# The second half of w_out, loaded behind a transpose instead of ahead of it

## The chip, the core and the metric

The kernel runs on one core of a Trainium2 chip. The metric is device time in microseconds (us): the time of one execution of the whole kernel on that core. A core has a matrix engine (TensorE, "PE" in the profile, with its weight loads as "PEld"), VectorE (DVE), ScalarE (ACT), GpSimd (POOL), and SyncE (SP), which in this kernel only issues transfers. Sixteen DMA engines move the data[...].

## The reference

The input x has 8 sequences of 4096 tokens with 192 channels. First comes a causal convolution over 7 tokens, with softmaxed taps that differ by head (8 heads of 24 channels). Then a two-layer network with the gate h * cos(h):

```
w   = softmax(weight)                          # 8 heads x 7 taps
c[s]= sum_k w[head, k] * x[s - 6 + k]          # zeros before a sequence starts
h   = c @ w_in                                 # 192 -> 2048
g   = h * cos(h)
out = g @ w_out                                # 2048 -> 192
```

All 32768 tokens go through it. The output is float32.

## The kernel before

The tokens are cut into 32 units of 1024 and, for the network, into 64 tiles of 512 (two tiles to a unit). For one unit the work is: load x (`load_unit`, L72, and `load_edges`, L68, both on SP's queue); cast it to bf16 (`cast_unit`, L178, mostly on GpSimd); convolve by matmuls with a banded matrix (`conv_mm`, L191) and copy the result to `ct` (`conv_out`, L200); transpose `ct` to `cT`, channels on the partitions, with a DMA transpose on SP's queue (`turn_unit`, L263); put right the first 6 tokens of each block (`mend_edges`, L283). The network then reads `cT`. In unit 0 the first half is transposed on TensorE (`turn_first`, L350) so that tile 0 can start early; its second half, which tile 1 reads, goes through the DMA transpose.

For one tile, `mm1` (L387) makes eight blocks of h, each 256 of the 2048 channels in a PSUM buffer of which there are three (`h_pool`). `gcu` (L399) has ACT compute the cosine (as a sine, L402) and DVE the product `g` (L406), after which the PSUM buffer is free again. `mm2_step` (L412) multiplies `g` by w_out (L439). It runs one tile behind `mm1`: during tile 1 it works on tile 0, and from its 17th step on it uses the second half of w_out.

w_out comes in float32 in two halves of two transfers each, 384 KB per transfer (`load_wo`, L94, on SP's queue), and each half is cast to bf16 on GpSimd (`cast_wo`, L91).

The order on TensorE is written out by hand, one string for a tile (`PE_FIRST` for the first four, then `PE_ORDER`), with `ACT_FIRST` and `ACT_ORDER` for ACT. "h3" is the fourth block of h, "m5" five steps of the second product, "c1 c2" and "d1 d2" parts of the convolution of later units, "r" the convolution of unit 0's second half:

```
PE_FIRST = ["h0a h0b h1 h2 h3 r h4 h5 d1 d2 h6 h7 c1 c2",
            "p h0 m5 h1 m5 h2 m6 h3 m12 h4 m2 h5 m2 q d1 d2 m5 h6 m6 c1 c2 m3 h7 m3",
```

In tile 1, d1 is the convolution of unit 2. "er" in ACT's string of tile 0 is the copy of "r" to `ct`; behind it stand the transpose of unit 0's second half and then, on SP, the loads of unit 2:

```
                    if k == "er":
                        turn_unit(0, NB, UB)
                        load_unit(2)
                        load_edges(2)
                        cast_wo(0)
```

After tile 0's string come, in program order, the copy of unit 1's `ct` (`double_unit`, L254), `cast_wo(1)`, the loads of unit 3 and the cast of unit 2. The transpose of unit 1 is issued in tile 1. SP works its list off in program order and stands where an entry waits; GpSimd does the same with its casts.

## Time and profile before

The time is 713.3 us, the median of three (713.25, 713.30, 715.74). The profiled execution spans 714.0 us.

| Engine | busy us | share of the span |
|---|---|---|
| TensorE (PE) | 703.3 | 99% |
| VectorE (DVE) | 646.7 | 91% |
| ScalarE (ACT) | 590.4 | 83% |
| GpSimd (POOL) | 300.9 | 42% |

| Transfers on SP's queue | count | KB each |
|---|---|---|
| x, whole units | 30 | 768 |
| x, half units | 4 | 384 |
| x, edges | 31 | 96 |
| w_out | 4 | 384 |
| transposes ct to cT | 32 | not listed |
| out | 63 | 384 |

A line of the timeline reads: start, duration, engine, line of the kernel, operation, output <- inputs, shape, count, and in brackets the idle time before it and what ended that. A line of the chain reads: start, duration, what the chain was in. A busy PE in these records is not PE at its peak, since the ends of matmuls are modelled.

### The profile page before, as it was taken

The page shows a single profiled execution, that of the slowest core. Times are in us where ns is not written, and L with a number is a line of the kernel's source. Part 1 is how long each engine was busy: PE and PEld are TensorE (multiplying, and loading weights), DVE is VectorE, ACT ScalarE, POOL GpSimd, SP SyncE. Part 2 cuts the span into 40 slices and gives each one's busy share as a digit, 9 for nine tenths or more (in the row PEclk, how much of TensorE's full clock was granted, in tenths as well). Part 3 has the DMA queues.
Part 4 walks back from the last instruction along what each step waited for, and adds up shares of the span by engine and source line. Part 5 has one row for each costly group of instructions (what it writes and reads, how often), then busy time and mean ns, then how long its engine had stood idle before and what let it go on. Part 6 is the DMA issues. An engine that isn't in the chain of part 4 may idle for free.

```text
span 714.0 us, 26519 instructions
## 1 busy us (share of the span) xinstructions
PE 703.3 (99%) x11828; PEld 538.3 (75%) x11829; DVE 646.7 (91%) x601; ACT 590.4 (83%) x719; POOL 300.9 (42%) x307
## 2 busy tenths in 40 slices
PE   7899999999999999999999999999999999999997
PEld 3577777777777777777777777777777777777776
DVE  7799999999999999999999999999999999999995
ACT  7788888888888888888888888888888888888774
POOL 6553345553245533445543355534355533453200
PEclk9999999999999999999999999999999999999999
DMA  8954553545644535544546534445535565513402
GB/s 213 232 110 115 145 127 100 138 94 127 146 104 115 142 86 137 146 107 113 126 94 146 144 97 124 113 107 145 137 91 138 98 122 145 122 52 92 95 25 68
DMA packets 183713, 85.25 MB, mean 119 GB/s; under 512 B 111664, under 2 KB 183216, under 8 KB 183600
## 3 DMA queue, kind: packets, MB, share of 16 engines
q1 hardware_dynamic: 182888, 82.59, 48.3%
q8 instruction: 92, 1.51, 0.9%
q0 software_dynamic: 416, 0.79, 0.8%
q14 instruction: 21, 0.17, 0.1%
q10 hardware_dynamic: 296, 0.20, 0.1%
HBM read 31.36 MB, written 25.17 MB: 79 GB/s over the span
## 4 chain that ended last, share of the span: by engine, by line
PE 96%; DVE 1%; DMA 1%; ACT 1%; issue 0%; POOL 0%; POOLq 0%; SPq 0%
PE o_ps L439 47%; PE h L395 46%; PE h L194 3%; DMA cT<-ct 1%; DVE g L406 0%; ACT cs L402 0%; PE h L439 0%; DVE band L320 0%; POOL mask L131 0%; ACT mask L136 0%; ACT ct L343 0%; PE o_ps L194 0%; DVE diag L309 0%; DVE cT L361 0%; PE h L358 0%
## 5 line engine op out<-in xcount | busy, mean ns | idle before, releaser
L406 DVE TENSOR_TENSOR g<-h,cs 128x1024 bf16<-128x1024 f32 (+1 forms) x513 | 606.4, 1220 | 32.3 <-ACT cs L402 21.8
L402 ACT ACTIVATE cs<-h 128x1024 bf16<-128x1024 f32 (+1 forms) x513 | 511.9, 1026 | 102.2 <-PE h L395 68.2
L439 PEld LDWEIGHTS <-g 64*128 64x128 bf16 x8192 | 369.5, 94 | 91.2 <-issue 1.2
L439 PE MATMUL o_ps<-wo,g 64*128 64x192 bf16 x8128 | 434.9, 243 | 0.0
L395 PE MATMUL h<-cT,w 64*128 64x512 bf16 (+1 forms) x3078 | 413.7, 376 | 4.7 <-DVE g L406 2.5
L395 PEld LDWEIGHTS <-w 64*128 64x128 bf16 x3078 | 161.1, 94 | 72.4 <-issue 4.8
L292 POOL TENSOR_TENSOR edge_prod<-cT,tap 128x1008 f32<-128x1008 bf16 x30 | 67.2, 2239 | 347.0 <-DMA cT<-ct 347.0
L183 POOL CAST x_bf<-x_f 128x1728 bf16<-128x1728 f32 (+2 forms) x33 | 80.6, 2444 | 6.7 <-DMA x_f<-in_x_dram 6.7
L209 ACT CAST ct<-h 128x384 bf16<-128x384 f32 x120 | 51.8, 483 | 8.5 <-PE h L194 4.8
L450 DVE COPY o_sb<-o_ps 128x384 f32<-128x384 f32 x63 | 35.2, 558 | 23.6 <-PE o_ps L439 23.2
L258 POOL COPY ct<-ct 128x1536 bf16<-128x1536 bf16 (+1 forms) x31 | 45.6, 1472 | 3.4 <-ACT ct L209 3.4
L194 PE MATMUL h<-x_bf,band 64*128 64x192 bf16 (+1 forms) x472 | 41.0, 243 | 0.0
L297 POOL TENSOR_TENSOR edge_prod<-edge_prod 128x144 f32<-128x144 f32 x60 | 33.3, 554 | 4.7
L295 POOL TENSOR_TENSOR edge_prod<-edge_prod 128x432 f32<-128x432 f32 x30 | 30.3, 1009 | 2.4
L450 ACT COPY o_sb<-o_ps 128x384 f32<-128x384 f32 x63 | 29.8, 473 | 1.6 <-PE o_ps L439 1.6
L194 PEld LDWEIGHTS <-band 64*128 64x128 bf16 (+1 forms) x496 | 24.7, 94 | 2.1 <-issue 1.0
L298 POOL TENSOR_TENSOR cT<-edge_prod 128x144 bf16<-128x144 f32 x30 | 18.3, 608 | 2.4
L260 POOL COPY ct<-x_bf 128x192 bf16<-128x192 bf16 x60 | 19.2, 349 | 0.0
L108 PE MATMUL o_ps<-zero 128*128 128x512 bf16 x12 | 4.7, 554 | 1.3 <-DVE zero L103 1.3
L108 PEld LDWEIGHTS <-zero 128*128 128x128 bf16 x15 | 1.6, 121 | 3.3 <-issue 1.9
L460 DVE COPY o_sb<-h 128x192 f32<-128x192 f32 x1 | 0.4, 358 | 3.7 <-PE h L439 3.7
L460 ACT COPY o_sb<-h 128x192 f32<-128x192 f32 x1 | 0.3, 319 | 3.8 <-PE h L439 3.8
(62 smaller groups left out, 43.3 us busy)
## 6 DMA issues: line engine op xcount, KB each, us to landing
out_dram<-o_sb SPq DMA_DIRECT2D x63, 384.0 KB
x_f<-in_x_dram SPq DMA_DIRECT2D x30, 768.0 KB
x_f<-in_x_dram SPq DMA_DIRECT2D x31, 96.0 KB
x_f<-in_x_dram SPq DMA_DIRECT2D x4, 384.0 KB
wo_f<-in_moe_w_out_dram SPq DMA_DIRECT2D x4, 384.0 KB
w<-in_moe_w_in_dram POOLq DMA_DIRECT2D x2, 384.0 KB, 6.3
cT<-ct SPq DMA_TRANSPOSE x32
out_dram<-o_sb ACTq DMA_DIRECT2D x2, 96.0 KB
```

The lines of the kernel that those rows point to most:

```text
L183: copy(out=bf[u][:, n0 + o : n1 + o, :].rearrange("p n (h k r) -> p (n h) k r", k=NC, r=R), in_=x_tiles[u][:, n0:n1, :].rearrange("p n (h ...
L194: return nc.tensor.matmul(out=ps[i // 2][:, 0 : (n1 - n0) * 2 * G].rearrange("p (n k i r) -> p i n k r", n=n1 - n0, k=NC, i=2)[:, i % 2], ...
L209: copy(o[:, :, 0, :], i[:, :, 0, :])
L258: nc.gpsimd.tensor_copy(out=ct[:, 0:nb, :, 1, :], in_=ct[:, 0:nb, :, 0, :])
L292: nc.gpsimd.tensor_tensor(out=edge_prod, in0=window, in1=tap.rearrange("p (a b k) -> p a b k", a=1, b=1).to_broadcast([128, NC * UB, K - 1 ...
L295: nc.gpsimd.tensor_tensor(out=edge_prod[:, :, :, 0:3], in0=edge_prod[:, :, :, 0:3], in1=edge_prod[:, :, :, 3:6], op=ALU.add)
L297: nc.gpsimd.tensor_tensor(out=edge_prod[:, :, :, 0], in0=edge_prod[:, :, :, 0], in1=edge_prod[:, :, :, j], op=ALU.add)
L395: nc.tensor.matmul(out=h[:, i, n0 * 128 : n1 * 128], lhsT=w[rows, k, j, :], rhs=c[rows, m0 + n0 : m0 + n1, k, :], start=(k == 0), stop=(k ...
L402: nc.scalar.activation(out=cs[:, :, part], in_=h[:, :, part], func=AF.Sin, bias=math.pi / 2.0, scale=1.0)
L406: nc.vector.tensor_tensor(out=g_tiles[t][:, 2 * j : 2 * j + 2, part], in0=h[:, :, part], in1=cs[:, :, part], op=ALU.mult)
L439: ms.append(nc.tensor.matmul(out=o_ps[tt, b, si], lhsT=g_tiles[tt][rows, f, s * 128 : (s + 1) * 128], rhs=wo[rows, f // 2, f % 2, :], star ...
L450: copies[b](o_sb[t][:, 2 * b : 2 * b + 2, :].rearrange("p s d -> p (s d)"), o_ps.pop((t, b)))
```

## The change

`load_wo(1)`, the two transfers of w_out's second half, is taken from the end of `conv_first` (after the conv of unit 0's first half) and put directly behind the transpose of unit 0's second half. In SP's queue and in the rings it then stands behind that transpose and ahead of the loads of unit 2. It is for letting the transpose, which tile 1 waits for, go ahead of data that are needed later. What is computed and what is transferred stays the same.

```diff
@@ -345,7 +345,6 @@
         tc.add_manual_dep(nc.sync.nop().ins, m.ins.name, sync_dep, reason="order of the transfers")
         load_wo(0)
-        load_wo(1)
 
     def turn_first(half):
         for n in range(2):
@@ -501,6 +500,7 @@
                     next(conv[k[1]], None)
                     if k == "er":
                         turn_unit(0, NB, UB)
+                        load_wo(1)
                         load_unit(2)
                         load_edges(2)
                         cast_wo(0)
```

## The prediction
> **What bounds the kernel now.** I read four views in this order: the page's chain of work, the chain in order of time for the first 40 us, the SP queue in order of time, and the DMA by stretch. The page says where the time is, and that nearly all of it cannot move:

> ```profile
> PE 96%; DVE 1%; DMA 1%; ACT 1%; issue 0%; POOL 0%; POOLq 0%; SPq 0%
> ```

> TensorE sets the end. The change touches only the start, so the question is where the chain leaves TensorE early on. The chain from 15 to 40 us:

> ```profile
> 16.79 5.64 DMA cT<-ct
> 22.43 0.05 issue
> 22.47 1.34 PE h L395 x6
> ...
> 37.41 1.24 DVE g L406
> 38.65 0.04 issue
> 38.69 0.82 PE h L395 x6
> ```

> From 16.79 to 22.43 the chain is the transpose of unit 0's second half ("transpose 0b"). From 38.69 on it is TensorE without a break to the end. So the change is worth what it moves that 38.69, and no more than what is lost before it. What waits there, in the timeline of TensorE:

> ```profile
> 22.47 1.34 PE L395 MATMUL h<-cT,w 64*128 64x512 bf16 x6 [2.02 <-DMA cT<-ct]
> ```

> And how TensorE fares afterwards, by stretch (busy us of PE, PEld, DVE, ACT, POOL, then granted clock, DMA share, GB/s):

> ```profile
> 19.22:22.63 3.41, 1.39 (x12) 0.57 (x13) 2.66 (x3) 2.96 (x5) 1.32 (x1) 1.00 0.68 135
> 22.63:26.05 3.42, 3.42 (x28) 1.90 (x26) 1.95 (x2) 1.14 (x2) 1.72 (x2) 0.50 1.06 316
> ```

> TensorE stands 2.02 us, and the 3.41 us after this stretch run at half clock. The rest of its idle time to 38.69 is two waits on VectorE (0.41 and 0.48) and crumbs. The most that can be had is thus 2.0 + 1.7 (half of 3.4) + 1.0 = 4.7 us, 0.66% of 713.3.

> Why is transpose 0b late? SP issues it at 16.79, 0.1 us after its input is complete; SP's timeline:

> ```profile
> 9.72 3.50 SPq L96 DMA_DIRECT2D wo_f<-in_moe_w_out_dram  x4
> 16.79 3.16 SPq L267 DMA_TRANSPOSE cT<-ct  x1
> ...
> 23.44 6.76 SPq L267 DMA_TRANSPOSE cT<-ct  x1
> ```

> So SP is not what holds it. The rings are, by stretch:

> ```profile
> 17.00:18.00 1.00, 0.38 (x4) 0.22 (x3) 1.00 (x2) 1.00 (x2) 0.63 (x1) 1.00 1.10 331
> 18.00:19.00 1.00, 0.82 (x6) 0.32 (x6) 1.00 (x1) 1.00 (x3) 0.84 (x1) 1.00 2.45 278
> 19.00:20.00 1.00, 0.84 (x7) 0.31 (x7) 1.00 (x2) 1.00 (x2) 0.00 (x0) 1.00 1.13 45
> 20.00:21.00 1.00, 0.46 (x4) 0.21 (x4) 0.89 (x2) 1.00 (x3) 0.00 (x0) 1.00 0.21 49
> 21.00:22.00 1.00, 0.00 (x0) 0.00 (x0) 0.57 (x1) 1.00 (x2) 0.69 (x1) 1.00 1.33 285
> ```

> Loads run at 330 GB/s until 18, and packets under 512 B, which are the transpose's, begin only then (at most 11 in any us from 14 to 17, 427 from 18 to 19). From 19.4 to 20.8 almost nothing moves: the finer slices of the DMA view show a plateau of about 20 GB/s, one engine's rate (a sixteenth of 330). One engine is still in its w_out packets, and the transpose makes no progress on the other fifteen. The likely cause of the lag stands in the DMA view from 17.0 to 18.2:

> ```profile
> q8 instruction: 1, 0.02, 5.7%
> ```

> One instruction packet of 16 KB, 5.7% of 16 engines for 1.2 us: 1.1 us of one engine.

> [...] Here a window with 1.39 of 3.41 us busy did so; the one before it, with 2.24 busy, did not. [...]

> **The change part by part.** It removes two issues of 393 KB from the end of the first x and w_out loads, and puts them between transpose 0b and the load of unit 2. Bytes and compute work stay the same.

> *Transpose 0b.* The rings carry 2.85 MB before it now (x 1.18 + 0.10, w_out 1.57) and 2.06 MB after, at 330 GB/s: they run dry 2.4 us sooner, at about 16, before the issue at 16.79. The price of a transpose on idle rings is that of the one issued at 58.39. The DMA view from 58.4 to 66, in 40 slices of 0.19 us:

> ```profile
> GB/s 0 0 0 0 0 0 90 216 222 217 199 217 218 218 217 216 218 222 217 213 220 217 216 212 216 220 182 220 330 422 323 315 307 299 93 8 12 16 24 24
> ```

> Its bytes begin 1.2 us after issue and flow at 217 GB/s. Transpose 0b has 393 KB, so 1.2 + 1.8 = 3.0 us, the last byte at 19.8. From last byte to TensorE it took about 0.65 us (21.8 to 22.47). Ready at 20.45 to 20.8 (the upper end if the 16 KB packet at 17.1, over at about 18.2, still holds one engine); I take 20.6. TensorE finishes its work at 20.45, so its wait shrinks from 2.02 to about 0.15: 1.9 us gained here. The window to 22.63 is then mostly busy, and the half-clock stretch goes.

> *w_out's second half.* It follows at 19.8: 786 KB / 330 = 2.4 us, landed at about 22.8. Its cast (1.47 us, L92) starts at 22.88 today, behind the ct copy on GpSimd, and so is hidden still; TensorE needs it in step m12, after the fourth h of tile 1, about 25.3 in the new schedule. Cost 0, bound 0.7.

> *What queues behind it.* Loads of units 2 and 3 and the transpose of unit 1 start 2.4 us later in the rings than without w_out, but the rings come free of transpose 0b 1.8 us earlier: net 0.6 later. SP's own issue time lies beside a backlog. So unit 2 lands by 26.85 (L183's cast starts at 26.25 now), and its cast of 2.55 ends at 29.4. Transpose 1's main flow starts at 29.5 (28.9 now), takes 2.85 as now, ends at 32.4. Now one late engine, after an instruction packet at 31.4, held its landing to 33.70. [...] other transposes of the trace with such a packet inside end 0.3 to 1.1 later than those without. Landing 33.2 to 34.3, I take 33.7, and the copy of 0.31 (L286) makes unit 1 ready at 34.1.

> *TensorE between.* Followed by hand with durations from the trace (h block 0.65, m step 0.082, ACT 1.04, DVE 1.22): h0 at 20.6, h1 at 21.8, h2 at 23.5 (its buffer is freed by DVE at 23.43), h3 at 24.7, h4 at 26.3, h5 at 27.15. It then reaches unit 2's conv (d1) at 28.0, where it waits for unit 2's cast until 29.4; now d1 stands at 30.78. From there to tile 2's first h it is 4.0 us by DVE, so 33.4, and that h needs unit 1: 34.1. Now it is at 35.50. Gain 1.4 us, carried on with the same ACT and DVE steps (3.2 us) to the block now at 38.69. The sum: 1.9 + 1.7 won at first, of which 2.2 are given back to the DVE ring, d1 and unit 1: 1.4 left. 713.3 - 1.4 = 711.9.

> **The rivals.** *Displacement*: the rings are conserved, and transpose 1 lands up to 1 us later than I think, so tile 2 starts at 35.1 to 35.5 again: 713.0 to 713.3. For it: TensorE had only 1.4 us of slack there (L286 done at 34.07, h at 35.50). Against: the dead 1.8 us in the rings from 19 to 20.8 goes. *Full carry*: the loads behind are quicker than my 0.6 shift and the instruction packet misses transpose 1; then unit 1 is ready by 33, DVE alone binds and 2.1 to 3.3 us stay: 711.2 to 710.0. Against: unit 2's cast at d1. *Slower*: with 0.5 to 2 us more delay of w_out, unit 2 or unit 1, TensorE pauses again in the window 26.05 to 29.46, of which my schedule fills only some 2.0 of 3.4 us (between the 1.39 that throttled and the 2.24 that did not); half clock to 32.87 takes 1.7 back and the late transposes more: 713.8 to 715. For it: the pause at d1 of 1.4 us. Against: it is shorter than the present 2.02.

> **How the numbers follow.** Forecast 0.50, displacement 0.22, full carry 0.15, slower 0.13. Predicted 711.9. The limits for 0.5% are 709.7 and 716.9. The cap of 4.7 us (708.6) means that faster by over 0.5% needs three quarters of everything lost: 0.06. Slower by 3.6 us would need two new pauses or a repetition like the 715.74 in the three times before: 0.06. Within: 0.88. Range: from the full carry's end, 710.0, to the slower case with the spread of the times before, 714.6.

> **What would show it.** Right: TensorE's wait for cT before tile 1 under 0.5 us; no half clock between 22.6 and 26; transpose bytes from 18.0 in one piece; w_out's second cast starting by 23.2; a new TensorE wait at d1 (on the cast L183) and one before tile 2's first h (on L286); TensorE unbroken from about 37.3. Wrong: a transpose that still ends after 21.5 (then its own pace, not the ring, was the limit), a cast of w_out after 24, a half-clock stretch after 29.46, or transpose 1 landing after 35.

## The result, and the profile after

| | median us | runs | ratio to before, 95% interval |
|---|---|---|---|
| before | 713.32 | 713.25 to 715.74 | |
| after | 717.64 | 716.80 to 718.47 | 1.0052 [1.0027, 1.0077] |

The change makes the kernel slower: the medians lie 4.3 us apart, and the ratio of the runs with its interval is 0.52%. The forecast was 711.9 with a range up to 714.6.

The execution of before whose profile stands ahead of the prediction is the one of 715.74 us, with a stretch at half clock; an execution of about the median has none: the same kernel profiled once more (run e1 below, 713.61 us) spans 711.9 us at full clock. Before is therefore taken from that one here. After spans 715.4 us (717.12 us), 3.5 us more.

The page's chain of after, by engine:

```profile
PE 95%; ACT 1%; DMA 1%; POOL 1%; SPq 1%; DVE 0%; issue 0%; POOLq 0%
```

Against before, SP's queue and GpSimd have come into it. The chain in order of time shows where (start, duration, what):

```profile
20.40 7.75 DMA x_f<-in_x_dram
28.15 0.02 issue
...
28.30 2.51 POOL x_bf L183
30.81 1.13 SPq L267
...
32.05 0.98 PE o_ps L438 x10
...
40.19 0.82 PE h L394 x6
```

The transpose of unit 0 is gone from it. In its place stands the load of unit 2, which ends at 28.15, then its cast, then SP's issue of unit 1's transpose. (The diff takes a line out, so that L395 of before is L394 here, and L439 is L438.) TensorE's timeline of after:

```profile
20.59 0.82 PE L394 MATMUL h<-cT,w 64*128 64x512 bf16 x6 [0.18 <-DMA cT<-ct]
...
30.85 0.49 PE L194 MATMUL h<-x_bf,band 128*128 128x192 bf16 x4 [2.83 <-POOL x_bf L183]
...
32.05 0.98 PE L438 MATMUL o_ps<-wo,g 64*128 64x192 bf16 x10 [0.68 <-SPq L167]
...
37.00 0.81 PE L394 MATMUL h<-cT,w 64*128 64x512 bf16 x6
```

The wait before tile 1, 2.02 or 1.63 us before, is 0.18 now. But unit 2's convolution (d1) waits 2.83 us for its input, and the step behind it 0.68 us for SP. For in this kernel SP does not only issue transfers: its list also holds entries that pass a signal on, and TensorE begins the second half of a tile's second product only when SP has passed on that the first half is done (`Turn`, L167). After the pause the granted clock is halved, by stretch:

```profile
27.90:31.31 3.41, 0.58 (x10) 0.52 (x6) 2.37 (x3) 1.12 (x2) 2.60 (x2) 1.00 1.33 156
31.31:34.72 3.41, 2.73 (x27) 1.76 (x26) 0.00 (x0) 1.29 (x4) 2.70 (x2) 0.50 1.13 256
```

The stretch with 0.58 of 3.41 us busy is followed by 3.41 us at half clock (0.50). The mean granted clock of this execution is 0.997; of the other three, two show 0.995 and one 0.998. One stretch of 3.41 us at half clock lowers the mean of 715 us by 0.0024, so two of the four executions had about two such stretches (worked out, not seen in a trace). Laid beside before at full clock, the loss can be followed mark by mark:

| TensorE starts, us | before (e1) | after | difference |
|---|---|---|---|
| first h of tile 1 | 22.13 | 20.59 | -1.54 |
| d1, unit 2's convolution | 28.76 | 30.85 | +2.09 |
| the step behind it (m5) | 29.72 | 32.05 | +2.33 |
| first h of tile 2 | 33.48 | 37.00 | +3.52 |
| third h of tile 2, TensorE unbroken from here | 36.67 | 40.19 | +3.52 |

The last row is the difference of the spans. In this pair of profiles 2.09 us are there at d1, 0.24 come with SP, and 1.19 behind it, where TensorE runs at half clock.

### The profile page after: what moved, and what is told of

Its sections match the earlier page's. It is cut to its first block, busy times and chain, and to the rows that moved or that the text cites. A ratio compares the mean times of both kernels' runs of the same rounds, so it can differ in the third digit from the quotient of the medians.

```text
span 715.4 us, 26520 instructions
## 1 busy us (share of the span) xinstructions
PE 703.6 (98%) x11829; PEld 537.3 (75%) x11829; DVE 646.2 (90%) x601; ACT 590.0 (82%) x719; POOL 300.6 (42%) x307
## 4 chain that ended last, share of the span: by engine, by line
PE 95%; ACT 1%; DMA 1%; POOL 1%; SPq 1%; DVE 0%; issue 0%; POOLq 0%
PE o_ps L438 47%; PE h L394 45%; PE h L194 3%; DMA x_f<-in_x_dram 1%; PE h L438 0%; ACT cs L401 0%; POOL x_bf L183 0%; DVE g L405 0%; SPq L267 0%; SPq L96 0%; ACT L151 0%; ACT x_bf L183 0%; POOL mask L131 0%; ACT mask L136 0%; PE o_ps L337 0%
## 5 line engine op out<-in xcount | busy, mean ns | idle before, releaser
L405 DVE TENSOR_TENSOR g<-h,cs 128x1024 bf16<-128x1024 f32 (+1 forms) x513 | 605.9, 1219 | 34.2 <-ACT cs L401 23.5
L438 PEld LDWEIGHTS <-g 64*128 64x128 bf16 x8192 | 368.8, 94 | 92.2 <-SPq L167 1.1
L438 PE MATMUL o_ps<-wo,g 64*128 64x192 bf16 x8128 | 434.6, 243 | 0.7 <-SPq L167 0.7
L394 PE MATMUL h<-cT,w 64*128 64x512 bf16 (+1 forms) x3078 | 412.8, 376 | 3.0 <-DVE g L405 2.6
L394 PEld LDWEIGHTS <-w 64*128 64x128 bf16 x3078 | 160.3, 94 | 71.0 <-issue 4.8
L183 POOL CAST x_bf<-x_f 128x1728 bf16<-128x1728 f32 (+2 forms) x33 | 80.3, 2436 | 7.8 <-DMA x_f<-in_x_dram 7.8
L449 DVE COPY o_sb<-o_ps 128x384 f32<-128x384 f32 x63 | 35.1, 557 | 23.8 <-PE o_ps L438 23.4
L297 POOL TENSOR_TENSOR edge_prod<-edge_prod 128x144 f32<-128x144 f32 x60 | 33.2, 554 | 4.7
L194 PEld LDWEIGHTS <-band 64*128 64x128 bf16 (+1 forms) x496 | 24.6, 94 | 4.9 <-issue 3.8
L298 POOL TENSOR_TENSOR cT<-edge_prod 128x144 bf16<-128x144 f32 x30 | 18.2, 608 | 2.4
```

The source lines that it names most:

```text
L183: copy(out=bf[u][:, n0 + o : n1 + o, :].rearrange("p n (h k r) -> p (n h) k r", k=NC, r=R), in_=x_tiles[u][:, n0:n1, :].rearrange("p n (h ...
L194: return nc.tensor.matmul(out=ps[i // 2][:, 0 : (n1 - n0) * 2 * G].rearrange("p (n k i r) -> p i n k r", n=n1 - n0, k=NC, i=2)[:, i % 2], ...
L297: nc.gpsimd.tensor_tensor(out=edge_prod[:, :, :, 0], in0=edge_prod[:, :, :, 0], in1=edge_prod[:, :, :, j], op=ALU.add)
L394: nc.tensor.matmul(out=h[:, i, n0 * 128 : n1 * 128], lhsT=w[rows, k, j, :], rhs=c[rows, m0 + n0 : m0 + n1, k, :], start=(k == 0), stop=(k ...
L405: nc.vector.tensor_tensor(out=g_tiles[t][:, 2 * j : 2 * j + 2, part], in0=h[:, :, part], in1=cs[:, :, part], op=ALU.mult)
L438: ms.append(nc.tensor.matmul(out=o_ps[tt, b, si], lhsT=g_tiles[tt][rows, f, s * 128 : (s + 1) * 128], rhs=wo[rows, f // 2, f % 2, :], star ...
```

## The experiments

The sizes below are in thousands of bytes, so that the 384 KB of a w_out transfer are 393 KB here.

Theory A: the transfers put ahead of unit 2 make it late; TensorE, which works in a written order, stands before unit 2's convolution, and the pause halves its clock. The rivals are named with each run. Each ratio is to the kernel before, measured beside the run.

**e1_before, e2_before_warm: what the half clock is worth before.** The first is the kernel unchanged. In the second, dummy matmuls of zeros (`keep_warm`, L106) fill the pause ahead of tile 1:

```diff
         h = h_pool.tile([128, 2, T], FP32, name="h")
+        if t == 1 and j == 0:
+            keep_warm(8, h[:, 0, :])
```

> The kernel before, unchanged, profiled once more. Theory A (the pause of 2.02 us before tile 1 halves the clock in some executions and not in others, by where it falls in the clock's windows): an execution of about 713.3 us shows a span near 711.6 and no half clock between 22 and 27 us, one of about 715.7 shows it. Theory B (the half clock is there in every execution of the kernel before, and the spread of 2.4 us has another source): half clock in each profile, whatever the time.

> The kernel before with 8 dummy matmuls of 512 columns put into the pause ahead of tile 1's first h, in its PSUM buffer. Theory A: no half clock in any execution, all times near 713.3 (at most 0.4 above, if the last dummy ends after the transpose lands). Theory B: times spread as before, 713.3 to 715.7, or all lower by the 1.7 us of the half clock, 711.6.

Measured: e1 713.67 us (713.04 to 715.89), profiled without half clock, span 711.9; e2 713.58 us (713.48 to 714.73), no execution above 715. The first lines of tile 1 and of d1 in TensorE's timeline of e1:

```profile
22.13 0.82 PE L395 MATMUL h<-cT,w 64*128 64x512 bf16 x6 [1.63 <-DMA cT<-ct]
...
28.76 0.51 PE L194 MATMUL h<-x_bf,band 128*128 128x192 bf16 x4
...
29.72 0.59 PE L439 MATMUL o_ps<-wo,g 64*128 64x192 bf16 x10 [0.42 <-SPq L167]
```

Theory A of these runs holds: the half clock comes in a minority of executions. The kernel before was executed 146 times beside the runs of this document. The 23 executions with a mean granted clock of 0.998 or less took 714.95 to 715.77 us, and the other 123 took 712.90 to 714.31. In the median there was no half clock to be won.

**e3_after_warm: the half clock after.**

```diff
         if whole:
+            if u == 2 and c == 0:
+                keep_warm(11, ps[0])
             for i in range(4):
```

> The changed kernel with 11 dummy matmuls of 512 columns ahead of unit 2's convolution (d1), in its PSUM buffer, where TensorE paused 2.83 us. Theory A (the changed kernel loses by the pause at d1 and the half clock that it brings): the half clock from 31.3 to 34.7 is gone, time 717.6 - 1.5 = 716.1 or lower, the start of tile 2 earlier by 1.5. Rival C (the wait of TensorE on SP's entry behind the transpose of unit 1 and that transpose itself set the start of tile 2): within 0.4 of 717.6.

Measured: 715.84 us, ratio 1.0037 [1.0024, 1.0050]; mean granted clock 0.999 or 1.000 in all five executions. Rival C falls. The half clock was worth 717.64 - 715.84 = 1.8 us between the medians (of four and five executions). The profiled execution, 716.68 us, lies above its median, and tile 2 starts only 0.47 us earlier in it than in after, not 1.5. What is left shows in TensorE's timeline of this run:

```profile
30.45 0.49 PE L194 MATMUL h<-x_bf,band 128*128 128x192 bf16 x4
...
32.87 0.59 PE L440 MATMUL o_ps<-wo,g 64*128 64x192 bf16 x10 [1.90 <-SPq L167]
```

TensorE came to m5 earlier and waited 1.90 us there for SP's entry. This entry stands in SP's list behind unit 1's transpose, and SP spends 7.77 us on issuing that. SP's timeline of the same run:

```profile
22.16 2.72 SPq L69 DMA_DIRECT2D x_f<-in_x_dram  x1
24.98 7.77 SPq L269 DMA_TRANSPOSE cT<-ct  x1
```

SP is done with it at 24.98 + 7.77 = 32.75, and TensorE goes on at 32.87. Part of the pause was thus filled by this second wait, which I had not put into the theory.

**e4_no_wo1: the transfer taken away.**

```diff
-                        load_wo(1)
...
-        nc.gpsimd.tensor_copy(out=wo[:, q * HP : (q + 1) * HP], in_=wo_f[:, q * HP : (q + 1) * HP])
+        nc.gpsimd.tensor_copy(out=wo[:, q * HP : (q + 1) * HP], in_=wo_f[:, 0:HP])
```

> The changed kernel without the transfer of w_out's second half; its cast reads the first half again, so that part of the second product uses the wrong half of w_out. Theory A (the 786 KB ahead of unit 2 cost its landing about 2 us): unit 2's cast starts by 26.0 instead of 28.3, TensorE's pause at d1 is under 1.2 us, no half clock, time 711.0 to 712.8. Rival D (unit 2 is late because of the transpose in front, or because SP is held up, and not because of w_out): cast still at 27.5 or later, time above 715.

Measured: 712.82 us, ratio 0.9990 [0.9982, 0.9999]. GpSimd's timeline has unit 2's cast at 24.66, where after has it at 28.30:

```profile
24.66 2.57 POOL L183 CAST x_bf<-x_f 128x1728 bf16<-128x1728 f32 x1 [0.30 <-DMA x_f<-in_x_dram]
```

TensorE has neither the pause at d1 nor the wait on SP; the 786 KB behind the transpose cost unit 2 3.6 us. Rival D falls. (Nor is it SP's time for issuing w_out's half: in after SP has issued unit 2's loads by 21.17, and w_out's cast still waits for its data until 23.58.) The run is also a ceiling for the idea in this schedule: with the transpose early and nothing behind it, only 0.57 us is won (713.39 - 712.82), because h2 of tile 1 then waits for VectorE (0.55 us in this run) and d1 moves by 0.74 us, from 28.76 to 28.02, not by 1.5.

**e5_warm_t1_later: the wait on SP taken away as well.** On top of e3:

```diff
             if k == "q":
+                if t == 1:
+                    turn_unit(1)
...
             if k == "p":
...
-                if t == 1:
-                    turn_unit(1)
```

> The changed kernel with the dummy matmuls of the run before, and with unit 1's transpose issued at the middle of tile 1 (behind SP's entry on which TensorE waits) instead of at its start. Theory A (of the 4.3 us lost, 1.8 are the half clock, 1 to 1.9 the wait on SP's entry behind the transpose's issue, and the rest the late unit 2): no wait on SP after d1, time 714.3 to 715.0, start of tile 2 at 34.9 to 35.5. Rival C (unit 1's transpose itself is what tile 2 waits for, and SP's entry costs nothing of its own): within 0.3 of the 715.84 with dummies alone, a wait of the first h of tile 2 on the mended unit 1.

Measured: 714.82 us, ratio 1.0016 [1.0008, 1.0024]; no wait on SP, the first h of tile 2 at 35.47 without a wait of its own. Without SP's entry the kernel is 1.0 us faster than e3, and Rival C falls. What is left is 1.25 us more than the kernel before, whose median beside this run was 713.57. In the profiled execution it is the late unit 2: its cast began at 28.78, and d1 waited for it until 31.35. But e8 and e9 below, where unit 2 holds TensorE up less, take 714.8 us as well, with unit 1's transpose issued as late as here. So this run doesn't show how much of the 1.25 us is unit 2's.

**e8_conv_later: TensorE no longer in order behind unit 2.**

```diff
-                "... h5 m2 q d1 d2 m5 h6 m6 c1 c2 m3 h7 m3",
+                "... h5 m2 q m5 h6 m6 h7 m3 d1 d2 c1 c2 m3",
```

with ACT's string to match and unit 1's transpose issued as in e5, without dummies.

> The changed kernel with unit 2's convolution (d, c) moved behind the last h of tile 1 on TensorE and ACT, and unit 1's transpose issued at the middle of tile 1. Theory A (the loss is TensorE standing in order behind a convolution that needs the late unit 2): no pause over 0.6 us in tile 1, no half clock; tile 2 then waits for unit 1 (its transpose ends no earlier than in the changed kernel, mended at about 34.1), starts at 34.1 to 34.5, time 714.0 to 714.6. If unit 1 is in time: 712.8 to 713.4. Rival C (unit 1 alone sets the loss): 715.8 or more.

Measured: 714.84 us, ratio 1.0016 [1.0009, 1.0023]. The pause at d1 is 0.67 us, and no half clock appears in the profiled execution. But the time is that of e5, because TensorE now waits for unit 1. TensorE's timeline:

```profile
31.32 0.49 PE L194 MATMUL h<-x_bf,band 128*128 128x192 bf16 x4 [0.67 <-POOL x_bf L183]
...
34.84 0.82 PE L394 MATMUL h<-cT,w 64*128 64x512 bf16 x6 [1.88 <-POOL cT L286]
```

Tile 2 stands 1.88 us for unit 1, whose transpose this run itself issues later. In the kernel before, the later issue alone brings the same wait (1.84 us, e10 below). So the run shows that most of the pause at d1 and, in the profiled execution, the half clock go when TensorE need not stand before unit 2, and that Rival C's 715.8 was not reached; it doesn't show that w_out's half costs anything beyond that.

**e6_half, e12_quarter, e7_wo1_behind_unit2: how much goes where.** In e6 one of the two transfers stays ahead of the transpose; in e12 590 KB stay ahead and 197 KB go behind; in e7 both go behind unit 2's loads. The edit shown is that of e6.

```diff
         load_wo(0)
+        load_wo(1, 0, 1)
...
                         turn_unit(0, NB, UB)
-                        load_wo(1)
+                        load_wo(1, 1, 2)
```

> Half of the change: of w_out's second half the first transfer (393 KB) stays ahead of the transpose of unit 0, the other goes behind it. Theory A (the rings have 2 us to spare ahead of the transpose, so that 393 KB there cost nothing, and each 393 KB behind it delay unit 2 by 1.5 us): TensorE's wait before tile 1 under 0.4 us, unit 2's cast starts at 26.0 to 26.6, pause at d1 0.3 to 1.2 us, no half clock, 712.9 to 714.2. Rival E (any w_out transfer directly behind the transpose holds up what follows, whatever its size): cast at 27.5 or later, time above 715.5.

> A quarter of the change: of w_out's second half 590 KB stay ahead of the transpose of unit 0 and 197 KB go behind it, so that the rings run dry just as its first packets come. Theory A (what is ahead is free up to the 2 us of slack in the rings, what is behind costs unit 2 about 1 us for 200 KB): TensorE's wait before tile 1 0.3 to 0.8, unit 2's cast starts at 25.2 to 25.8, d1 at 28.0 to 28.5, a wait on SP's entry of 0.5 to 1, 712.9 to 713.5, the same as before within the measurement. Rival H (an instruction packet again leaves one engine behind, and any w_out packet ahead holds the transpose): wait before tile 1 above 1.2, times spread up to 715.7.

> The changed kernel with the loads of unit 2 ahead of w_out's second half. Theory A (it is the order in the rings that makes unit 2 late): unit 2 lands by 24.6, but w_out's second half only at 27.5 to 28.5, and GpSimd's casts stand in order behind it: w_out's cast 27.5 to 30, unit 2's cast 29 to 32.5; TensorE pauses 3 to 4 us at step m12, half clock behind it, time 717 to 720. Rival F (the rings serve by size or interleave, the order counts little): as the changed kernel, 717.6 within 0.5.

| run | KB behind the transpose, ahead of unit 2 | wait before tile 1 | unit 2's cast at | us | ratio, 95% interval |
|---|---|---|---|---|---|
| before (e1) | 0 | 1.63 | 25.54 | 713.67 | 1.0006 [1.0000, 1.0013] |
| e12 | 197 | 1.31 | 26.19 | 713.77 | 1.0006 [0.9998, 1.0015] |
| e6 | 393 | 0.46 | 26.48 | 713.98 | 1.0010 [1.0000, 1.0021] |
| after | 786 | 0.18 | 28.30 | 717.64 | 1.0052 [1.0027, 1.0077] |
| e4 | 0, not loaded | 0.19 | 24.66 | 712.82 | 0.9990 [0.9982, 0.9999] |
| e7 | 0, behind unit 2 | 0.20 | 28.43, behind w_out's | 717.49 | 1.0054 [1.0039, 1.0069] |

Unit 2's cast comes the later the more goes ahead of it (25.54, 26.19, 26.48 and 28.30 us with 0, 197, 393 and 786 KB), and the wait before tile 1 is the shorter the less of w_out's second half goes ahead of the transpose (1.63, 1.31, 0.46 and 0.18 us). The times of before, e12 and e6 are not told apart by their intervals; after and e7 are clearly slower. e6 already takes away most of the wait before tile 1, yet is no faster, since 393 KB ahead of unit 2 give the gain back, at d1 and on SP's entry, on which the expectation had not counted. TensorE's timeline of e6:

```profile
29.07 0.49 PE L194 MATMUL h<-x_bf,band 128*128 128x192 bf16 x4 [1.13 <-POOL x_bf L183]
...
31.56 0.59 PE L439 MATMUL o_ps<-wo,g 64*128 64x192 bf16 x10 [1.97 <-SPq L167]
```

(The profiled executions of e3, e5, e6 and e12 lie 0.7 to 1.4 us above the medians of these runs, so that the waits seen there are rather at their upper end.) Four of the 20 executions of e6 took 716.4 to 717.5 us at a mean granted clock of 0.997 or 0.998; its profiled one has no half clock. Rival E falls: 393 KB behind cost much less than 786. In e12 Theory A missed: the wait before tile 1, unit 2's cast and the wait on SP's entry (1.69 us) all came out larger than expected, and the time is 0.27 us above its range. The 1.31 us before tile 1 lie just above Rival H's limit of 1.2; whether an engine was left behind was not shown. In e7 the cast of w_out is late instead, at 27.02 where after has 23.58, and TensorE waits for it at m12:

```profile
28.54 1.17 PE L438 MATMUL o_ps<-wo,g 64*128 64x192 bf16 x24 [3.20 <-POOL wo L92]
```

Theory A is right there in the wait and the time. (The profiled execution, 716.09 us, has no half clock; the other three, 717.5 to 718.4 us, have mean clocks of 0.995 to 0.998.) The time is as bad as after, for another reason than Rival F's: not that the order counts little, but that w_out's half has a due time of its own.

**e9_half_t1_later, e10_before_t1_later: unit 1's transpose later, on the half change and on before.** The edit is that of e5.

> Half of the change (one w_out transfer behind, one ahead), with unit 1's transpose issued at the middle of tile 1, behind SP's entry. Theory A (in the half change SP's entry cost TensorE 1.97 us and unit 2's cast 1.13): no wait on SP, start of tile 2 at 33.3 to 33.9, 712.9 to 713.6, level with the kernel before; executions above 715 become rare. Rival C (unit 1's transpose sets the start of tile 2 anyway): 713.9 to 714.6.

> The kernel before with unit 1's transpose issued at the middle of tile 1. Theory A (where unit 2 is in time, SP's entry costs 0.4 us at most, and the later issue costs as much): 713.0 to 713.7, same. Rival C (the later issue delays unit 1, which tile 2 waits for): 714.0 or more.

Measured: e9 714.77 us, ratio 1.0017 [1.0011, 1.0024]; e10 715.27 us, 1.0024 [1.0015, 1.0034]. Theory A missed both. Rival C named the wait, though e9 lies 0.17 us above its range. The wait on SP is gone, but tile 2 waits for the mended unit 1; the lines are from TensorE's timelines of e9 and of e10:

```profile
34.62 0.82 PE L395 MATMUL h<-cT,w 64*128 64x512 bf16 x6 [1.36 <-POOL cT L286]
37.64 0.82 PE L395 MATMUL h<-cT,w 64*128 64x512 bf16 x6 [1.84 <-POOL cT L286]
```

A transpose issued at the middle of tile 1 comes too late, even where nothing else does. (The profiled execution of e10, 717.81 us, is one with half clock and lies 2.5 us above the median.) At its old place this transpose holds up TensorE's entry, at the middle of tile 1 it holds up tile 2.

**e11_reordered: an attempt at a version that beats both.** On top of e6: unit 1's transpose ahead of unit 3's loads, those at the middle of tile 1, the mending of unit 1 ahead of unit 3's cast, and the convolutions of units 2 and 3 later on TensorE and ACT.

```diff
             double_unit(1)
+            turn_unit(1)
             cast_wo(1)
-            load_unit(3)
-            load_edges(3)
             cast_unit(2)
...
-                "m5 h0 c1 m10 p c2 h1 h2 m7 h3 ...
+                "m5 h0 m10 p h1 h2 c1 c2 m7 h3 ...
```

> A version from the findings: one w_out transfer ahead and one behind, unit 1's transpose issued ahead of unit 3's loads, these at the middle of tile 1, the mending of unit 1 ahead of unit 3's cast on GpSimd, and the convolutions of units 2 and 3 later on TensorE and ACT. Theory A (the start is bound by VectorE's ring once no load is late): tile 2 starts at 32.5 to 33.1, 712.4 to 713.0, 0.05% to 0.15% below before. Rival G (unit 3, now loaded behind the transpose, is late for its convolution in tile 2): a pause of 0.5 us or more there, 713.4 or more.

Measured: 722.18 us, ratio 1.0118 [1.0104, 1.0131]. The start came out as expected: SP issues unit 1's transpose at 22.89 in 4.47 us, nothing waits for SP in tile 1, and tile 2 starts at 32.74, 0.74 before e1's. So with unit 3's loads out of its way there is a place where this transpose holds up neither. Then TensorE stands before and in the middle of unit 3's convolution, where its halves change banks:

```profile
36.76 0.34 PE L194 MATMUL h<-x_bf,band 64*128 64x192 bf16 x4 [1.08 <-POOL x_bf L183]
43.57 0.50 PE L194 MATMUL h<-x_bf,band 64*128 64x192 bf16 x4 [6.47 <-SPq L167]
```

The entry on SP for this change of banks now stands behind the next transpose, which SP issued from 38.72 to 42.82, and a store, and TensorE waits 6.47 us for it; the clock is halved (0.50) from 40.5 to 47.3 us. Rival G's pause (1.08) is there too. No run beats the kernel before with its full work: e2, e6 and e12 are level with it at best. Unit 3's loads directly behind the transpose at its place in e11, with TensorE's order as in before, were not tried, so whether a faster version exists stays open.

## Why the prediction was wrong, by its steps

*Transpose 0b*: right. Predicted ready at 20.6 by the price of a later transpose on idle rings; TensorE went on at 20.59. The DMA view of after from 17 to 20 us, in 40 slices, shows its bytes in one piece, most of them at 198 to 229 GB/s, where that price had 217:

```profile
GB/s 0 0 0 0 0 0 0 0 0 0 0 0 0 27 116 201 222 222 229 201 222 205 229 198 208 201 215 215 229 215 215 218 215 177 154 198 212 239 178 171
```

*The base of the sum*: wrong. The gain of 1.4 us was reckoned on a profile of the execution of 715.74 us, the slowest of three, and was then taken off 713.3, the median of the three. The 1.7 us of half clock that it counted as won are not there in most executions. The forecast's own marks show it: TensorE was to run unbroken from about 37.3 us, which is 1.4 before the 38.69 of that profile but 0.6 after the 36.67 of e1. Beside an execution at full clock, the schedule that was forecast was itself a small loss.

*w_out's second half*: roughly right. Its cast began at 23.58, against 22.88 before and at most 23.2 by the forecast; nobody waited for it in after. Its bytes began at about 20.5, not 19.8.

*What queues behind it*: this is the step that failed in the run itself, first in a size and then in a wait that it left out. "Net 0.6 later" was to put unit 2's cast at 26.85; it began at 28.30, 2.05 after the profile it was reckoned from, and 2.8 after e1. The step had two terms. That the rings come free of transpose 0b 1.8 us earlier was about right: in e4, without w_out's half, the cast began at 24.66, 1.6 us before the 26.25 of the profile. The price of the 786 KB was not: 2.4 us at the mean rate was forecast, and it was 3.6 from e4 to after. In e3, e5 and e8, which have the same transfers there, the cast began 3.0 to 4.1 us after e4's. e7 has it the other way round: unit 2's 885 KB ahead of w_out's half put that one's cast back by 3.4 us, where the mean rate gives 2.7.

From 20 to 28 us after moved 271 and 310 GB/s, about 2.3 MB, while w_out's half and unit 2 together are 1.67 MB: by this estimate, from the mean rates of two stretches, some 0.65 MB of what SP had issued behind unit 2 had moved before unit 2's cast began at 28.30. The DMA view of after from 28.5 to 32 us, in 40 slices, shows what came next:

```profile
GB/s 222 237 222 217 380 167 167 138 123 61 61 44 44 35 53 35 53 41 53 41 50 47 47 29 29 26 20 249 293 281 290 301 287 293 281 290 301 287 293 281
```

For about 1.5 us only 20 to 61 GB/s move, before unit 1's transpose flows at 249 to 301. By an estimate, with a sixteenth of the 330 GB/s of before as one engine's rate, that is the work of one to three engines. That the engines end a load at different times is my reading of it; these views hold all engines together and don't show it.

The second error stands in the sentence "SP's own issue time lies beside a backlog": TensorE's own step waits for SP's list, 0.42 us in e1 already, 0.68 in after and 1.90 when e3 fills the pause. Unit 1's transpose was priced well: its mending began at 34.05, and 34.1 was forecast for its end. It was not what tile 2 waited for.

*TensorE between*: the hand-made schedule was good up to d1, where TensorE arrived at 28.0 as forecast; it then waited to 30.85 and not to 29.4. From d1 to tile 2 it took 6.15 us and not 4.0, with the wait on SP and the half clock; in e5, with neither, it took 4.12.

*The rivals*: the slower one named the mechanism, a second pause, with half clock behind it, though I gave it 0.13 and a size of 0.5 to 1.7 us. It reckoned with some 2.0 of 3.4 us busy in the window of the pause; it was 0.58. One of the signs of being wrong came true, a half-clock stretch after 29.46 (from 31.31).

Of the 5.7 us between 711.9 and 717.64, 2.0 are thus the base (38.69 - 36.67), and 2.9 are unit 2, SP and the half clock (40.19 - 37.3). The rest, 0.8, is how far the two profiled executions lie from the medians. How the loss parts into late unit 2, SP's entry and half clock depends on the order in which they are taken away. The medians of e3 and e5 give 1.8 for the half clock and 1.0 for SP's entry, and leave 1.4 (1.25 beside e5's own before). These three add up to the whole by construction, which proves nothing about the parts. What is shown is that all of it goes when the 786 KB are not ahead of unit 2 and nothing takes their place (e4).

## What to carry to other kernels

Moving a transfer out of the way of one consumer can move it into the way of the next: work out the due time of everything behind it, not by the mean rate alone (786 KB were 2.4 us by it here and 3.6 us in the runs), and test the ceiling with the transfer left out, which here was 0.57 us. A queue that also carries synchronization entries can make a long issue on it a wait for the engine that needs these entries: here 0.42 to 6.47 us. And before a feature of one profile is counted as gain, see whether the median execution has it, and take the gain off the time of the execution that was profiled.

## What the runs showed of the hardware

```profile
26.13:29.54 3.41, 2.28 (x32) 1.49 (x26) 3.19 (x4) 2.19 (x3) 2.81 (x2) 1.00 1.23 252
29.54:32.95 3.41, 1.44 (x27) 1.04 (x26) 0.87 (x1) 1.04 (x4) 2.23 (x1) 1.00 1.31 175
```

The longer pause did not bring the half clock where the shorter one did: the 3.20 us of e7 fell into two windows with 1.54 and 2.10 us busy, and the clock stayed at 1.00; the 2.02 us of before fell into one, with 1.39. In e1, the same kernel, the pause of 1.63 us left 1.79 us busy in its window, and the clock stayed at 1.00. Since the ends of matmuls are modelled, the busy times are approximate.

Issuing the same transpose, unit 1's, took SP 4.15 us in e10, from 31.17, where 44 GB/s moved from 29.71 to 33.12, and 7.77 us in e3, from 24.98, where 312 GB/s moved from 24 to 28.
